# A recurrent layer and two MLPs: router products shared between VectorE and TensorE, a gate product moved to GpSimd, one operation for the decay of the states

## The chip, the cores and the metric

The kernel runs on one core of a Trainium2 chip. The core's engines work side by side, each through its own queue in order: TensorE (PE, with its weight loads as PEld), VectorE (DVE), ScalarE (ACT), GpSimd (POOL) and SyncE (SP), which only issues DMAs here. The metric is the time of one execution in microseconds (us); lower is better.

## The reference

Three layers in a row: a recurrent attention with a matrix state per head, an MLP with the activation h - tanh(h), and a mixture of eight experts in which each token goes to the expert with the largest normalised product.

```python
for t in range(S):                       # B=4, H=8, S=768, D=40
    ...
    C = f_stab * C + i_stab * np.einsum('bhd,bhe->bhde', vt, kt)
    n = f_stab[:, :, None] * n + i_stab[:, :, None] * kt
    h_tilde = np.einsum('bhde,bhe->bhd', C, qt)
    denom = np.maximum(np.abs(nq), 1.0)
    o = 1.0 / (1.0 + np.exp(-o_gate[:, :, t]))
    y[:, :, t] = o * h_tilde / denom
...
h = x @ w_in                             # x: 3072 x 320, w_in: 320 x 2048
return ((h - np.tanh(h)) @ w_out)
...
xn = x / (np.linalg.norm(x, axis=-1, keepdims=True) + 1e-06)
en = expert_emb / (np.linalg.norm(expert_emb, axis=-1, keepdims=True) + 1e-06)
logits = xn @ en.T / tau                 # 3072 x 8
expert_idx = np.argmax(logits, axis=1)
...
out[mask] = gate_w[mask, None] * (np.maximum(x[mask] @ w1[e], 0.0) @ w2[e])
```

## The kernel before, in words

The sequence of 768 is cut into six chunks of 128 (`NCH`), and a chunk of one batch is a unit, so there are 24 units i = 4c + b. Within a unit the attention is worked out for the whole chunk at once; from chunk to chunk only the states `Cst` are carried, one 40 x 41 block per head, two heads side by side in the partitions 0 to 39 and 64 to 103 (columns 0 to 40 and 41 to 81) with zeros in the other blocks.

A unit has these steps, each placed at a step of the main loop by `PLACE1` (chunk 1) and `PLACE2` (chunks 2 to 5): `parts` (split of q and k into a high part on ACT and a low part on DVE or POOL, L162), `scores` (matmuls into `ps`, L562 or L564, exponentials on ACT, a mask on POOL), `weigh` (product with the mask into `A`, L580), `outs` (matmuls into `po` and `pi`), `sums` (sums `tmp` L617 and `T` L620, the denominator `dn` with its reciprocal, the gate product `z` = sigmoid(o) x 1/dn L630, the decay of the states L640 and their update L642), `finish` (`y` = T x z, L645 and L647), `turn` (transposes of y into `px` on PE), `low` (the copy of `px` as input of the first MLP, and the store of y). `stack` copies the states in high and low parts for the next chunk (`Cl`, L162 on POOL).

The first MLP runs over the six chunks (512 tokens each) as six stages of 16 steps n, one block of 128 hidden units a step: `gemm1` (8 matmuls into one of two PSUM banks `h`), `g_chain` (u and s on ACT, L210 and L211; s and g on DVE, L212 and L213, which reads `h` and so frees the bank), `g_split` (`ghi` on ACT, `glo` on POOL), `gemm2` (12 matmuls into four banks `acc`). In step n the loop issues the split of n + 1, the chain of n + 2, `gemm2` of n and `gemm1` of n + 3. In stage c the attention of chunk c + 1 runs beside it, and the routing of chunk c - 1. After stage 5 come ten passes over the experts with 8 steps each.

The routing (`route`, then `slots`) takes the four tiles of 128 tokens of a chunk. For each it forms the squared norm on ACT and eight products with the experts' vectors: `VDOT[c]` of them on DVE (one operation each with a running sum, L263, from a copy `enb` of the vectors in every partition), the others as a product on POOL (L267) with the sum on ACT (L268). `VDOT` 0 means `dots`: the tile is transposed on PE (three matmuls into `pd`, L241), copied to `xt` (DVE L242, ACT L243), and multiplied with the transposed vectors `enT` (three matmuls, L246), and DVE copies the eight columns (L247). Chunk 5 alone does so; it is routed after stage 5. `enT` is made by `turn_en`: a load of the 8 x 320 vectors `es` into a buffer of z's tag, three transposes into one bank `pn` on PE, three copies on ACT. `slots` is a generator; each step of the main loop runs it to its next `yield`.

The instructions of the start-up are written in their order by hand; from the `|` in `START` on a scheduler orders them by its own costs, with the code's order as priority. So a change of one part can shift the order of others. The buffers of a pool's tag are used in turn, and an instruction that needs one waits for the last user of the one before.

Of the kernel before, what the change touches and what calls it, by code (L numbers as in the profile page):

```python
# [9 lines left out]
F32 = mybir.dt.float32  # L10
# [5 lines left out]
AF = mybir.ActivationFunctionType  # L16
ALU = mybir.AluOpType
# [5 lines left out]
NCH = S // L  # L23
# [4 lines left out]
E = 8  # L28
# [25 lines left out]
STACK = 12  # L54
SIGM = (2, 14)
EXPERT_X = (-3, 0)
LOAD_EW, LOAD_X, LOAD_X2, TURN_EN = 13, 4, 4, 6
KW_POOL = (0, 2, 3, 4, 5)
VDOT = (8, 8, 8, 8, 6, 0)
WARM0, WARM = 20, 2  # L60


# [48 lines left out]
def build(ctx, tc, qk, qk3, vk, og, gat, w64, w12, emb, tau, cst, tok, empty, out):  # L111
    nc = tc.nc
    V, A, G, T = nc.vector, nc.scalar, nc.gpsimd, nc.tensor
    MM = T.matmul

    const = ctx.enter_context(tc.tile_pool(name="const", bufs=1))
# [105 lines left out]
    enT = []  # L222

    def turn_en():

        e8 = attp.tile([8, 320], F32, tag="z", name="e8", bufs=1)
        nc.sync.dma_start(out=e8, in_=es)
        pn = at_bank("pn")
        enT.append(attp.tile([128, 3, 8], F32, tag="dn", name="enT"))
        for k in range(3):  # L230
            n = min(128, 320 - 128 * k)
            T.transpose(pn[0:n, 8 * k:8 * k + 8], e8[:, 128 * k:128 * k + n], ident[0:8, 0:8])
            A.activation(out=enT[0][0:n, k, :], in_=pn[0:n, 8 * k:8 * k + 8], func=AF.Copy)

    def dots(x2, lg):

        pd = at_bank("pd")
        xt = attp.tile([128, 384], F32, tag="y", name="xt")
        for k in range(3):
            n = min(128, 320 - 128 * k)  # L240
            T.transpose(pd[0:n, 128 * k:128 * k + 128], x2[:, 128 * k:128 * k + n], ident)  # L241
        V.tensor_copy(out=xt[:, 0:256], in_=pd[:, 0:256])  # L242
        A.activation(out=xt[0:64, 256:384], in_=pd[0:64, 256:384], func=AF.Copy)  # L243
        for k in range(3):
            n = min(128, 320 - 128 * k)
            MM(pd[:, 384:392], xt[0:n, 128 * k:128 * k + 128], enT[0][0:n, k, :], start=k == 0, stop=k == 2)  # L246
        V.tensor_copy(out=lg, in_=pd[:, 384:392])  # L247

    def slots(pool, nj, R, si, vdot=E, part=E):

        n = nj * 8
        ss = pool.tile([128, nj], F32, tag="ss", name="ss")
        lg = pool.tile([128, nj, 8], F32, tag="lg", name="lg")
        jk = [pool.tile([128, 320], BF16, tag=f"jk{k}", name="jk") for k in range(2)]
        for j in range(nj):
            x2 = R[:, j, 0:320]
            A.activation(out=jk[0], in_=x2, func=AF.Square, accum_out=ss[:, j:j + 1])
            if vdot == 0:
                dots(x2, lg[:, j, :])
                yield  # L260
            for e in range(E if vdot else 0):
                if e < vdot:
                    V.scalar_tensor_tensor(out=jk[1], in0=x2, scalar=1.0, in1=enb[:, e, :], op0=ALU.mult, op1=ALU.mult,  # L263
                                           accum_out=lg[:, j, e:e + 1])
                else:
                    dt = attp.tile([128, 320], F32, tag="A", name="dt")
                    G.tensor_tensor(out=dt, in0=x2, in1=enb[:, e, :], op=ALU.mult)  # L267
                    A.activation(out=jk[0], in_=dt, func=AF.Copy, accum_out=lg[:, j, e:e + 1])  # L268
                if (e + 1) % part == 0:
                    yield  # L270
        G.tensor_tensor(out=ss, in0=ss, in1=half[:, 0:nj], op=ALU.pow)
        V.tensor_scalar(out=ss, in0=ss, scalar1=1.0e-6, scalar2=None, op0=ALU.add)
        V.reciprocal(out=ss, in_=ss)
        yield
        V.tensor_scalar(out=ss, in0=ss, scalar1=itau, scalar2=None, op0=ALU.mult)
        V.tensor_tensor(out=lg, in0=lg, in1=ss.unsqueeze(2).to_broadcast([128, nj, 8]), op=ALU.mult)
        mx = pool.tile([128, nj, 1], F32, tag="mx", name="mx")
        V.tensor_reduce(out=mx, in_=lg, op=ALU.max, axis=AX.X)
        eq = pool.tile([128, nj, 8], F32, tag="eq", name="eq")
        V.tensor_tensor(out=eq, in0=lg, in1=mx.to_broadcast([128, nj, 8]), op=ALU.is_ge)  # L280
        V.tensor_tensor(out=lg, in0=lg, in1=mx.to_broadcast([128, nj, 8]), op=ALU.subtract)
        A.activation(out=lg, in_=lg, func=AF.Exp)
        wt = col(C_WT, n).rearrange("p (j e) -> p j e", j=nj)
        V.tensor_tensor(out=eq, in0=eq, in1=wt, op=ALU.mult)
        V.tensor_reduce(out=mx, in_=eq, op=ALU.max, axis=AX.X)
        V.tensor_tensor(out=eq, in0=wt, in1=mx.to_broadcast([128, nj, 8]), op=ALU.is_equal)
        oh = pool.tile([128, nj, 8], BF16, tag="oh", name="oh")
        pre = pool.tile([128, nj, 8], BF16, tag="pre", name="pre")
        V.tensor_copy(out=oh, in_=eq)
        V.tensor_copy(out=pre[:, 0, :], in_=carry)  # L290
        for j in range(1, nj):
            V.tensor_tensor(out=pre[:, j, :], in0=pre[:, j - 1, :], in1=oh[:, j - 1, :], op=ALU.add)
        V.tensor_tensor(out=carry, in0=pre[:, nj - 1, :], in1=oh[:, nj - 1, :], op=ALU.add)
        yield
        pr = at_bank("pr")
        MM(pr[:, 0:n], trib, oh.rearrange("p j e -> p (j e)"), start=True, stop=False)
        MM(pr[:, 0:n], oneb, pre.rearrange("p j e -> p (j e)"), start=False, stop=True)
        gs = pool.tile([128, nj, 1], F32, tag="gsum", name="gsum")
        V.tensor_reduce(out=gs, in_=lg, op=ALU.add, axis=AX.X)
        V.tensor_scalar(out=gs, in0=gs, scalar1=1.0e-9, scalar2=None, op0=ALU.add)  # L300
        V.reciprocal(out=R[:, :, 320:321], in_=gs)
        sl = pool.tile([128, nj, 8], F32, tag="sl", name="sl")
        V.tensor_tensor(out=sl, in0=pr[:, 0:n].rearrange("p (j e) -> p j e", j=nj),
                        in1=col(C_EOFF, n).rearrange("p (j e) -> p j e", j=nj), op=ALU.add)
        V.tensor_tensor(out=sl, in0=sl, in1=eq, op=ALU.mult)
        V.tensor_reduce(out=mx, in_=sl, op=ALU.add, axis=AX.X)
        V.tensor_copy(out=si, in_=mx.rearrange("p j o -> p (j o)"))
        yield
# [63 lines left out]
    attp = p1.enter_context(tc.tile_pool(name="attp", bufs=2))  # L372
# [3 lines left out]
    Cst = attp.tile([104, 16, 82], F32, tag="C", name="C", bufs=1)  # L376
    gts = {}
    units = {}
    sig = {}
# [3 lines left out]
    eGL = attp.tile([104, NCH * 16], F32, tag="eGL", name="eGL", bufs=1)  # L383
# [143 lines left out]
    def attention(c):  # L527
# [3 lines left out]
        def unit(b):  # L531
            i = c * B + b
# [76 lines left out]
            def sums():  # L609
# [5 lines left out]
                if c:  # L615
                    Tt = v['T'] = attp.tile([128, 8, 41], F32, tag="T", name="T", bufs=1)
                    V.tensor_tensor(out=tmp, in0=po[:, 0:w * 8].rearrange("p (h d) -> p h d", h=8)[:, :, 0:41],  # L617
                                    in1=eG[:, 8 * i:8 * i + 8].unsqueeze(2).to_broadcast([128, 8, 41]),
                                    op=ALU.mult)
                    V.tensor_tensor(out=Tt.rearrange("p h d -> p (h d)"), in0=pi[:, 0:328],  # L620
                                    in1=tmp.rearrange("p h d -> p (h d)"), op=ALU.add)
                else:
                    Tt = v['T'] = pi[:, 0:328].rearrange("p (h d) -> p h d", h=8)
                dn = attp.tile([128, 8, 1], F32, tag="dn", name="dn")
# [2 lines left out]
                V.tensor_tensor(out=dn, in0=nq, in1=dn, op=ALU.max)  # L627
                V.reciprocal(out=dn, in_=dn)
                z = v['z'] = attp.tile([128, 8, 40], F32, tag="z", name="z", bufs=1)
                (V if c > 1 else G).tensor_tensor(out=z, in0=sig[i].rearrange("p (h d) -> p h d", h=8),  # L630
                                                  in1=dn.to_broadcast([128, 8, 40]), op=ALU.mult)
                if c == 0:
                    for par in range(2):
                        p0, c0 = 64 * par, 41 * par
                        A.activation(out=Cst[p0:p0 + 40, 4 * b:4 * b + 4, c0:c0 + 41], in_=st[p0:p0 + 40, :, :],
                                     func=AF.Copy)
                for par in range(2 if 0 < c < NCH - 1 else 0):
                    p0, c0 = 64 * par, 41 * par
                    Cv = Cst[p0:p0 + 40, 4 * b:4 * b + 4, c0:c0 + 41]
                    V.tensor_tensor(out=Cv, in0=Cv, in1=eGL[p0:p0 + 40, 4 * i:4 * i + 4].unsqueeze(2)  # L640
                                    .to_broadcast([40, 4, 41]), op=ALU.mult)
                    V.tensor_tensor(out=Cv, in0=Cv, in1=st[p0:p0 + 40, :, :], op=ALU.add)  # L642
            def finish():
                y = v['y'] = attp.tile([128, 384], F32, tag="y", name="y")
# [30 lines left out]
        for b in range(B if c else 0):  # L675
            n = 16 * (c - 1) - 4 + 4 * b
# [140 lines left out]
    NS = NCH * NF  # L817
# [8 lines left out]
    for word in START.split():  # L826
        op, k = word[0], word[1:]
# [126 lines left out]
            sp[n] = relu_chain(hs.pop(n), rows_of(step(n)[0])[3])  # L954

    def special(n, c, f, rx):
        if n == NS - TURN_EN:
            turn_en()
        if n == NS - NF - 4:
            ranking()  # L960
# [34 lines left out]
    for n in range(NS + NE):  # L995
        c, f, ps = step(n)
# [51 lines left out]
        elif f == NFE - 1:  # L1048
            ti, gt = exT[c][3:5]
            for j, bank in enumerate(acc.pop(('e', c))):  # L1050
# [4 lines left out]
                        in_=ob[0:m], in_offset=None, bounds_check=NT - 1, oob_is_err=False)  # L1055
# [26 lines left out]
    with tc.If(reg > CAP):  # L1082
        X = gp.tile([128, XW], F32, tag="X", name="X")
        xt = gp.tile([128, 3, 128], F32, tag="xt", name="xt")
# [150 lines left out]
```

## Time and profile before

| what | value |
| --- | --- |
| time of the runs | 851.04 us median of 3 (850.98 to 857.43) |
| the profiled execution | 854.08 us, span 852.1 us from first to last instruction |
| mean granted TensorE clock | 0.927 of full speed |
| busy, share of the span | PE 90%, PEld 80%, DVE 75%, ACT 58%, POOL 43% |
| stages 0 to 5 begin at (first matmul of `gemm1`) | 58.8, 162.4, 262.6, 360.0, 451.6, 536.2 us |
| the expert passes' first `gemm1` | 611.0 us |

The stretches in the tables run from one of these starts to the next. A row of busy time counts the time in which at least one instruction of the engine ran; matmuls overlap each other, and at the lower of the two clock levels they take longer, so a busy PE is not the same as a PE at full speed. A row of waits names the instruction that waited, the one that released it, the sum in us, the number of times and the longest.

### The profile page before, as it was taken

To read this page: it belongs to the slowest core of one execution; us is meant where nothing else is said; L and a number is where in the kernel's file an instruction comes from. 1 tells how busy PE (TensorE), PEld (TensorE's weight loads), DVE (VectorE), ACT (ScalarE), POOL (GpSimd) and SP (SyncE) were. 2 spreads that over 40 slices of the span, in tenths; PEclk is the share of its full clock that TensorE was granted. 3 is DMA by queue.
4 is the path that set the end of the run, shared out by engine and by line. 5 is a ranking of instruction groups with operands and counts; after the bars stand their busy time and mean duration, and the time that the engine had idled before them with its cause. 6 is when DMAs were issued, how large, how long until landed. Compare 5 with 4: busy or idle time off the path is not lost. (4 is left out here: it accounts for less than half of the span.)

```text
span 852.1 us, 14301 instructions
## 1 busy us (share of the span) xinstructions
PE 763.0 (90%) x4640; PEld 677.6 (80%) x4640; DVE 638.1 (75%) x1417; ACT 496.1 (58%) x1175; POOL 364.3 (43%) x375
## 2 busy tenths in 40 slices
PE   8979899797899898998889989888899999999994
PEld 5767778686788687787778778767799989999994
DVE  6476999898887989879986999797473775556420
ACT  3775787767557645685558634655554655455421
POOL 2383677657463554655463525443522111012111
PEclk8558998988989989999999999999999999999998
DMA  8574766543344243432335311201535764455000
GB/s 273 211 254 160 257 220 198 133 122 93 87 126 131 82 101 87 143 105 79 89 109 152 92 34 44 73 1 51 177 115 164 232 181 140 120 173 165 36 20 21
DMA packets 60756, 107.55 MB, mean 126 GB/s; under 512 B 24958, under 2 KB 33321, under 8 KB 60016
## 3 DMA queue, kind: packets, MB, share of 16 engines
q1 hardware_dynamic: 57968, 98.46, 38.8%
q0 software_dynamic: 2512, 7.89, 2.5%
q8 instruction: 38, 0.62, 0.3%
q14 instruction: 46, 0.38, 0.1%
q10 hardware_dynamic: 192, 0.20, 0.1%
HBM read 92.91 MB, written 17.87 MB: 130 GB/s over the span
## 5 line engine op out<-in xcount | busy, mean ns | idle before, releaser
L185 PE MATMUL h<-xh,wi 128*128 128x512 f32 (+6 forms) x880 | 303.3, 382 | 18.8 <-DVE g L213 13.3
L185 PEld LDWEIGHTS h<-xh,wi 128*128 128x128 f32 x880 | 171.7, 198 | 45.7 <-DVE g L213 17.3
L193 PE MATMUL acc<-wo,ghi 128*128 128x320 f32 (+1 forms) x616 | 200.6, 326 | 0.0
L162 POOL TENSOR_TENSOR glo<-g,ghi 128x512 fp32r<-128x512 f32 x96 | 133.2, 1389 | 156.6 <-ACT ghi L218 119.8
L185 PE MATMUL h<-xl,wi 128*128 128x512 f32 (+6 forms) x528 | 197.7, 379 | 0.4
L195 PE MATMUL acc<-wo,glo 128*128 128x320 f32 (+1 forms) x616 | 194.9, 317 | 2.0 <-POOL glo L162 2.0
L194 PE MATMUL acc<-wo,ghi 128*128 128x320 f32 (+1 forms) x616 | 194.7, 316 | 0.0
L218 ACT ACTIVATE ghi<-g 128x512 fp32r<-128x512 f32 x96 | 60.2, 628 | 111.7 <-DVE g L213 94.6
L193 PEld LDWEIGHTS acc<-wo,ghi 128*128 128x128 f32 (+1 forms) x616 | 118.4, 192 | 6.1 <-ACT D L568 1.3
L195 PEld LDWEIGHTS acc<-wo,glo 128*128 128x128 f32 (+1 forms) x616 | 117.7, 191 | 4.0 <-POOL glo L162 3.2
L194 PEld LDWEIGHTS acc<-wo,ghi 128*128 128x128 f32 (+1 forms) x616 | 118.1, 192 | 3.2
L185 PEld LDWEIGHTS h<-xl,wi 128*128 128x128 f32 x528 | 105.0, 199 | 12.3 <-DVE xl L660 1.6
L212 DVE SCALAR_TENSOR_TENSOR s<-s,u 128x512 f32<-128x512 f32 x96 | 78.9, 822 | 41.8 <-ACT s L211 40.2
L263 DVE SCALAR_TENSOR_TENSOR jk<-R,enb 128x320 bf16<-128x320 f32 x152 | 96.5, 635 | 2.7 <-ACT R L727 1.7
L156 POOL DMA_INDIRECT out<-ob,ti x29 | 28.5, 982 | 156.9 <-ACT ob L1053 133.3
L929 DVE SCALAR_TENSOR_TENSOR glo<-h,ghi 128x256 fp32r<-128x256 f32 (+5 forms) x80 | 41.4, 517 | 60.0 <-ACT ghi L928 54.5
L568 ACT ACTIVATE D<-D,bcol 128x128 f32<-128x128 f32 x192 | 64.6, 390 | 33.6 <-DMA D<-gd 33.3
L928 ACT ACTIVATE ghi<-h 128x256 fp32r<-128x256 f32 (+5 forms) x80 | 36.7, 458 | 65.4 <-PE acc L194 55.9
L162 DVE TENSOR_TENSOR wi<-ew,wi 128x256 fp32r<-128x256 f32 (+1 forms) x128 | 50.1, 392 | 31.4 <-ACT wi L174 29.8
L211 ACT ACTIVATE s<-u,cs 128x512 f32<-128x512 f32 x96 | 68.7, 716 | 0.9
L213 DVE SCALAR_TENSOR_TENSOR g<-s,h 128x512 f32<-128x512 f32 x96 | 65.4, 682 | 2.9
L210 ACT ACTIVATE u<-h 128x512 f32<-128x512 f32 x96 | 55.9, 583 | 12.6 <-PE h L185 11.3
(192 smaller groups left out, 1199.5 us busy)
## 6 DMA issues: line engine op xcount, KB each, us to landing
ew<-in_w SPq DMA_DIRECT2D x64, 352.0 KB
W<-in_qk SPq DMA_DIRECT2D x32, 480.0 KB
D<-gd SPq DMA_DIRECT2D x48, 256.0 KB
raw<-in_w SPq DMA_DIRECT2D x16, 704.0 KB
vk<-in_vk SPq DMA_DIRECT2D x20, 324.0 KB
xs<-blank SPq DMA_DIRECT2D x32, 161.0 KB
sg<-in_og SPq DMA_DIRECT2D x6, 640.0 KB
ys<-y SPq DMA_DIRECT2D x24, 160.0 KB
```

The lines of the kernel that those rows point to most:

```text
L162: eng.tensor_tensor(out=out, in0=x, in1=hi.bitcast(F32), op=ALU.subtract)
L185: MM(h[:, 0:cols], wi[:, k, :], x[:, kk, :], start=n == 0, stop=n == len(seq) - 1)
L193: MM(o, ghi[:, sl], wo[:, 0, 0:320], start=first, stop=False)
L194: MM(o, ghi[:, sl], wo[:, 1, 0:320], start=False, stop=False)
L195: MM(o, glo[:, sl], wo[:, 0, 0:320], start=False, stop=last)
L210: A.activation(out=u, in_=h, func=AF.Square, accum_out=usum[:, n:n + 1])
L211: A.activation(out=s, in_=u, func=AF.Square, bias=col(C_BETA))
L212: V.scalar_tensor_tensor(out=s, in0=s, scalar=GAMMA, in1=u, op0=ALU.add, op1=ALU.mult)
L213: V.scalar_tensor_tensor(out=g, in0=s, scalar=C2, in1=h, op0=ALU.mult, op1=ALU.mult)
L218: A.activation(out=ghi, in_=g, func=AF.Copy)
L263: V.scalar_tensor_tensor(out=jk[1], in0=x2, scalar=1.0, in1=enb[:, e, :], op0=ALU.mult, op1=ALU.mult, accum_out=lg[:, j, e:e + 1])
L568: A.activation(out=Dt[:, j, :], in_=Dt[:, j, :], func=AF.Exp, bias=bcol[:, k:k + 1])
```

## The change

Five edits. In the chunks 0 to 4 the tiles 0 and 2 of the four now go through `dots`, the tiles 1 and 3 have all eight products on DVE (`VDOT[4]` is 8 instead of 6, so nothing is left for POOL and ACT there); a tile in `dots` has one `yield` instead of two. Since `enT` is needed from chunk 0's routing on, `turn_en` stands at step 12 instead of step 90, and `enT` has a buffer of its own. The larger copy to `xt` is ACT's instead of DVE's. The product `z` is on POOL for all chunks (before: chunks 0 and 1). The decay of a unit's states is one operation over 104 partitions and both halves of the columns instead of one for each block of 40 partitions.

```diff
-LOAD_EW, LOAD_X, LOAD_X2, TURN_EN = 13, 4, 4, 6
+LOAD_EW, LOAD_X, LOAD_X2, TURN_EN = 13, 4, 4, 12
 KW_POOL = (0, 2, 3, 4, 5)
-VDOT = (8, 8, 8, 8, 6, 0)
+VDOT = (8, 8, 8, 8, 8, 0)
...
-        enT.append(attp.tile([128, 3, 8], F32, tag="dn", name="enT"))
+        enT.append(const.tile([128, 3, 8], F32, tag="enT", name="enT"))
...
-        V.tensor_copy(out=xt[:, 0:256], in_=pd[:, 0:256])
+        A.activation(out=xt[:, 0:256], in_=pd[:, 0:256], func=AF.Copy)
         A.activation(out=xt[0:64, 256:384], in_=pd[0:64, 256:384], func=AF.Copy)
...
-            if vdot == 0:
+            on_pe = vdot == 0 or part < E and j % 2 == 0
+            if on_pe:
                 dots(x2, lg[:, j, :])
                 yield
-            for e in range(E if vdot else 0):
+            for e in range(0 if on_pe else E):
...
-                (V if c > 1 else G).tensor_tensor(out=z, in0=sig[i].rearrange("p (h d) -> p h d", h=8),
+                G.tensor_tensor(out=z, in0=sig[i].rearrange("p (h d) -> p h d", h=8),
...
+                if 0 < c < NCH - 1:
+                    Cu = Cst[:, 4 * b:4 * b + 4, :]
+                    V.tensor_tensor(out=Cu, in0=Cu, in1=eGL[:, 4 * i:4 * i + 4].unsqueeze(2).to_broadcast([104, 4, 82]), op=ALU.mult)
                 for par in range(2 if 0 < c < NCH - 1 else 0):
...
-                    V.tensor_tensor(out=Cv, in0=Cv, in1=eGL[p0:p0 + 40, 4 * i:4 * i + 4].unsqueeze(2)
-                                    .to_broadcast([40, 4, 41]), op=ALU.mult)
                     V.tensor_tensor(out=Cv, in0=Cv, in1=st[p0:p0 + 40, :, :], op=ALU.add)
...
-        if n == NS - TURN_EN:
+        if n == TURN_EN:
             turn_en()
```

Below, the order of the instructions at three places, first before and then after. A row is line, operation, output<-inputs and shape; lines after the edits are shifted by one or two (L263 becomes L264, L630 L631, L645 L647).

PE in the fourth step of stage 2, in `gemm2` (L193 to L195, banks `acc`), before:

```order
L194 MATMUL acc_2948<-wo,ghi 128x320
L195 MATMUL acc_2948<-wo,glo 128x320
L193 MATMUL acc_2949<-wo,ghi 128x320
L194 MATMUL acc_2949<-wo,ghi 128x320
L195 MATMUL acc_2949<-wo,glo 128x320
L193 MATMUL acc_2950<-wo,ghi 128x320
L194 MATMUL acc_2950<-wo,ghi 128x320
L195 MATMUL acc_2950<-wo,glo 128x320
L185 MATMUL h<-xh,wi 128x512
```

And after, where the third tile of chunk 1 goes through `dots`:

```order
L194 MATMUL acc_2955<-wo,ghi 128x320
L195 MATMUL acc_2955<-wo,glo 128x320
L241 MATMUL pd<-cs,R 128x128 x2
L241 MATMUL pd<-cs,R 64x128
L193 MATMUL acc_2956<-wo,ghi 128x320
L194 MATMUL acc_2956<-wo,ghi 128x320
L195 MATMUL acc_2956<-wo,glo 128x320
L193 MATMUL acc_2957<-wo,ghi 128x320
L194 MATMUL acc_2957<-wo,ghi 128x320
L246 MATMUL pd<-enT,xt 128x8 x3
L195 MATMUL acc_2957<-wo,glo 128x320
L185 MATMUL h<-xh,wi 128x512
```

Transposes and products stand inside `gemm2`, five of its matmuls apart, and `gemm1` (L185) follows.

DVE at the end of a unit's `sums` in stage 1 (dn the denominator, q the low parts of a later unit's q), before:

```order
L627 TENSOR_TENSOR dn<-T,dn 128x8
L642 TENSOR_TENSOR C<-C,po 40x4x41
L628 RECIPROCAL dn<-dn 128x8
L162 TENSOR_TENSOR q_2410<-W,q_2410 40x512
L630 TENSOR_TENSOR z<-sg,dn 128x320
L162 TENSOR_TENSOR q_2488<-W,q_2488 40x512
L645 TENSOR_TENSOR y<-T,z 128x320
L212 SCALAR_TENSOR_TENSOR s<-s,u 128x512
```

And after:

```order
L628 TENSOR_TENSOR dn<-T,dn 128x8
L162 TENSOR_TENSOR q_2441<-W,q_2441 40x512
L629 RECIPROCAL dn<-dn 128x8
L162 TENSOR_TENSOR q_2528<-W,q_2528 40x512
L647 TENSOR_TENSOR y<-T,z 128x320
L304 TENSOR_TENSOR sl<-pr,cs 128x32
L649 COPY y<-y 128x64
```

z has left this queue; y follows the reciprocal with one operation between. On POOL z stands after:

```order
L162 TENSOR_TENSOR glo<-g,ghi 128x512
L162 TENSOR_TENSOR Cl<-C,C_1612 40x164
L631 TENSOR_TENSOR z<-sg,dn 128x320
L156 DMA xs<-R,si 24576x322 x4
L162 TENSOR_TENSOR glo<-g,ghi 128x512
```

It has come in between the low parts `Cl` of the states and `glo` (L156 are the scatters of the routing).

PE at step 12, in the last `gemm2` rows of that step (px the transposes of y of the last unit of chunk 1), after; before, these rows hold neither pn nor its waits, and `turn_en` stood in stage 5:

```order
L195 MATMUL acc_761<-wo,glo 128x320
L232 MATMUL pn<-cs,e_1646 128x8
L655 MATMUL px<-cs,y 128x128 x3
L193 MATMUL acc_762<-wo,ghi 128x320
L232 MATMUL pn<-cs,e_1646 128x8
L194 MATMUL acc_762<-wo,ghi 128x320
L195 MATMUL acc_762<-wo,glo 128x320
L232 MATMUL pn<-cs,e_1646 64x8
L185 MATMUL h<-xh,wi 128x512
```

The three transposes of `turn_en` now stand between matmuls of `gemm2`, the first of them ahead of px.

## Rows read from the trace of the kernel before

**Rows 1.** Busy time by stretch, whole core, stages 1 to 5 in order:

```profile
core 0: us, PE busy (x) PEld busy (x) DVE busy (x) ACT busy (x) POOL busy (x), PEclk, DMA share, GB/s
...
162.38:262.64 100.26, 86.83 (x529) 77.14 (x528) 85.45 (x197) 62.38 (x150) 59.95 (x59) 0.90 0.41 113
262.64:360.01 97.37, 84.97 (x529) 74.64 (x528) 84.41 (x193) 60.19 (x141) 51.19 (x50) 0.93 0.38 103
360.01:451.62 91.61, 82.28 (x528) 72.27 (x528) 82.95 (x185) 60.16 (x141) 47.97 (x48) 0.96 0.38 103
451.62:536.17 84.55, 76.13 (x457) 66.38 (x456) 74.67 (x184) 49.54 (x113) 36.40 (x29) 1.00 0.25 72
536.17:610.95 74.78, 65.00 (x332) 54.43 (x333) 57.19 (x131) 44.15 (x113) 35.04 (x33) 0.98 0.18 57
```

**Rows 2.** Waits of PE, stage 1 (waiter, releaser, us, times, longest):

```profile
PE ps L564 <- DVE q L162: 9.3, 2, 5.3
PE ps L564 <- DVE k L162: 2.3, 2, 1.8
```

**Rows 3.** The same view, engine PE, stage 4:

```profile
PE ps L564 <- DVE k L162: 2.5, 3, 1.1
```

**Rows 4.** The same view, engine PE, stage 5:

```profile
PE h L185 <- DVE g L213: 7.8, 7, 3.3
...
PE pn L232 <- ACT enT L233: 1.1, 1, 1.1
```

**Rows 5.** Busy time of L263 alone (products on DVE) in stages 1 to 5:

```profile
162.38:262.64 100.26, 19.19 (x64) 0.90 0.41 113
262.64:360.01 97.37, 18.89 (x64) 0.93 0.38 103
360.01:451.62 91.61, 22.43 (x64) 0.96 0.38 103
451.62:536.17 84.55, 20.68 (x64) 1.00 0.25 72
536.17:610.95 74.78, 16.56 (x48) 0.98 0.18 57
```

**Rows 6.** Groups of instructions by shape, whole run (xcount, busy us, mean ns):

```profile
L640 DVE TENSOR_TENSOR C<-C,eGL 40x164 f32<-40x164 f32 x32 | 17.3, 540 | 5.8 <-PE po L592 4.7 <-POOL Cl L162 0.6
...
L617 DVE TENSOR_TENSOR tmp<-po,eG 128x328 f32<-128x328 f32 x20 | 9.9, 493 | 2.9 <-remote 2.2 <-PE po L596 0.6
...
L630 DVE TENSOR_TENSOR z<-sg,dn 128x320 f32<-128x320 f32 x16 | 12.7, 795 | 0.2
...
L630 POOL TENSOR_TENSOR z<-sg,dn 128x320 f32<-128x320 f32 x8 | 7.2, 894 | 12.4 <-DVE dn L628 12.4
```

**Rows 7.** L645 in stage 0, then whole run: duration ns min/median/max, who waited:

```profile
L645 DVE TENSOR_TENSOR y<-T,z x4: 809/1278/1559, 82.0 to 154.7; 128x320 f32<-128x320 f32 x4
...
  PE px L653: 4.7, 2
...
L645 DVE TENSOR_TENSOR y<-T,z x20: 475/491/1574, 82.0 to 531.0; 128x320 f32<-128x320 f32 x20
```

**Rows 8.** L212 and L213 in the whole run: duration ns min/median/max:

```profile
L212 DVE SCALAR_TENSOR_TENSOR s<-s,u x96: 672/686/1783, 65.7 to 610.1; 128x512 f32<-128x512 f32 x96
...
L213 DVE SCALAR_TENSOR_TENSOR g<-s,h x96: 669/681/690, 66.9 to 611.1; 128x512 f32<-128x512 f32 x96
```

**Rows 9.** Timeline around chunk 5's products on PE (start us, us, engine, what):

```profile
621.15 0.81 PE L241 MATMUL pd<-cs,R 128*128 128x128 f32 x6
...
622.84 0.93 PE L246 MATMUL pd<-enT,xt 128*128 128x8 f32 x6
...
624.22 0.17 DVE L247 COPY lg<-pd 128x8 f32<-128x8 f32 x1 [1.12 <-ACT wo L175]
```

**Rows 10.** Timeline of SP's queue at the write and re-read of es:

```profile
60.20 0.29 SPq L719 DMA_DIRECT2D es<-em  x1
...
64.25 0.32 SPq L720 DMA_DIRECT2D enb<-es  x1
```

## The prediction, made before the changed kernel was timed

> **What bounds the kernel now.** I read the table of stretches first, because the change acts on five of them. A stage is sixteen steps of the first MLP, cut at the first matmul of `gemm1` (L185) of every sixteenth step. Look at PE's column and the clock beside it [rows 1]. Stage 1 lasts 100.3 us with PE busy for 86.8 at a granted clock of 0.90, that is partly at 1.2 instead of 2.4 GHz. A clock that is 0.10 short costs at most 0.10 x 100.3 = 10.0 us, so the same PE work at full clock needs about 76.8 us. I call this the floor and the rest, 23.5 us, the excess. The same sum gives floors of 78.2, 78.6, 76.1 and 63.5 us for stages 2 to 5 and excesses of 19.2, 13.0, 8.4 and 11.3.
>
> DVE's column says where the excess comes from. DVE is busy for 85.5, 84.4, 83.0, 74.7 and 57.2 us [rows 1]; divided by the floor that is 1.11, 1.08, 1.06, 0.98 and 0.90. The excess falls with this ratio until about 1 and then stays near 8 to 11. The waits of PE agree: in stage 1 the scores (L564) wait 9.3 and 2.3 us for DVE's low parts of q and k [rows 2], of 13.4 us that PE is idle at all (100.26 - 86.83). In stage 4 the largest is still a DVE wait, 2.5 us [rows 3]. In stage 5, where no attention is left, `gemm1` waits 7.8 us for g (L213), because its PSUM bank comes free only behind DVE's queue [rows 4]. So stages 1 to 3 are bound by a DVE that works through more than PE does; stages 4 and 5 by PE with stalls in the pipeline. The expert passes behind stage 5 are not touched.
>
> **The change part by part.**
>
> *Products.* L263 takes 19.2, 18.9, 22.4 and 20.7 us of DVE in stages 1 to 4 for 32 products each, and 16.6 us for 24 in stage 5 (the count in the rows includes the read of each sum) [rows 5]. Two of four tiles leave DVE, so half goes in stages 1 to 4: 9.6, 9.4, 11.2 and 10.3 us. In stage 5 `VDOT` rises from 6 to 8 for the tiles that stay, so 24 become 16 and 5.5 us go, and with them eight products on POOL and eight sums on ACT, which nobody waited for long. Two copies of 0.17 us per stage come in (L247) [rows 9].
>
> *The same products on TensorE.* Chunk 5 already does this, so the price is in the trace: six transposes, two tiles', in 0.81 us, and one tile's three products, each recorded twice, in 0.93 us [rows 9]. One tile costs 0.81 / 2 + 0.93 = 1.34 us of PE, two tiles 2.7 us a stage. This is added to the floors of all five stages. The two copies of the transposed tile now both run on ACT; the order puts five products of `gemm2` between transposes and products to cover them. I take the cover as enough; without it each tile stalls PE, which is the third rival.
>
> *Decay of the states.* 32 operations of 540 ns become 16 over 104 partitions and 328 columns [rows 6]. That shape is not in the trace as such. 493 ns is what L617 takes for 328 columns with one input in PSUM [rows 6]; an operation with both inputs in SBUF is stretched at times (L212 against L213 [rows 8]), so I take 0.7 us, between 0.49 and twice 0.54. 17.3 - 16 x 0.7 = 6 us of DVE, about 2 us in each of stages 0 to 2, where the decays of four chunks lie (bounds: 17.3 - 16 x 1.08 = 0, and 17.3 - 16 x 0.49 = 9.4).
>
> *Gate product z on POOL.* It takes 795 ns on DVE and 894 ns on POOL [rows 6]. But DVE does not simply win 16 x 0.8 us. Where z is on POOL already (stage 0), the y behind it takes 1278 ns in the median against 491 ns over the run [rows 7]. 795 - (1278 - 491) is zero, so I take nothing for DVE and 1 us in total for later y's. The reason shows elsewhere too: L212, with both inputs in SBUF, is stretched from 686 to as much as 1783 ns, while L213, which has one input in PSUM, never leaves 669 to 690 [rows 8]. The Trainium skill, SBUF — State Buffer, section "SBUF: two separate sides", says that a DVE operation with two SBUF inputs and a GpSimd operation exclude each other for a whole instruction. By that rule moving z to POOL frees no DVE time, and the trace agrees; whoever credits DVE with the full 12.7 us, and PE with all of it, comes to about 820 instead of 834.
>
> *Turning the experts' vectors (`turn_en`) early.* Its load of 10 KB now waits on SP for y of the last unit of chunk 1, because it takes z's only buffer; behind it on SP wait that unit's store of y, which waits for the same y anyway, and a load of W. PE meets the first transpose between two banks of `gemm2`, ahead of that unit's px, and must wait for the load. The nearest row: es is written from 60.20 and its re-read, which needs it landed, is issued at 64.25, so such a transfer lands within 4.1 us [rows 10]. Two turnarounds with ACT follow, 1.1 us where PE waited for one [rows 4]. Bounds 0 and 6.3; I take +3 in stage 0. In stage 5 the 1.1 us go.
>
> **Sum.** DVE falls to 74.2, 73.3, 72.1, 64.7 and 52.0 us, at most 0.93 of the new floors (79.5, 80.9, 81.3, 78.8, 66.2). Below a ratio of 1 the trace shows an excess of 8.4 (stage 4), so I give this to stages 1 to 3, which also means that almost no time at the low clock is left there. Stage 4 has a seventh less DVE work before its waits: 7.0. Stage 5 loses 1.1 and a part of its waits for g: 9.0. New stages: 87.9, 89.3, 89.7, 85.8, 75.2, against before -12.4, -8.1, -1.9, +1.3, +0.4; together -20.7. With +3 for `turn_en` and +1 for z: -17. The profiled execution took 854.1 us (span 852.1), the median of the runs is 851.0; 17 us off the median is **834 us**.
>
> The gain sits in stages 1 and 2. What is late next is PE itself: 80 of 88 us in each stage.
>
> **Bounds.** If less DVE work also halves the excess of stage 4, to 4.2, and that of stage 5 to 5.6, and `turn_en` and z cost nothing, the stages give 83.7, 85.1, 85.5, 83.0 and 71.8: -39.5, about 811. If the excess falls only half the way to 8.4 (16.0, 13.8, 10.7), stays in stage 4 and is 10.2 in stage 5, they give 95.5, 94.7, 92.0, 87.2, 76.4: -2.8, and with `turn_en` at 6 it is 854.
>
> **Rivals.**
>
> *z's new path takes the relief back (no change).* Before, reciprocal, z and y followed each other on DVE. Now DVE reaches y while z stands in POOL's queue behind `glo` and `Cl`, and px on PE needs y. In stage 0 this cost PE 4.7 us in four units [rows 7], 1.2 us each; sixteen units more would cost 19 us, so 834 + 19 - 1 = 852. For it: POOL is busy for 60 of 100 us in stage 1, and the stage will be shorter. Its y is longer there as well: 16 x (1278 - 491) ns is 12.6 us ahead of px, 834 - 1 + 12.6 = 846 by that alone [rows 7]. Against it: stage 0 also has the weights' conversion on DVE, and one other operation still stands between reciprocal and y. The lock of the Trainium skill (the page and section named above) would stretch y in just this way, since T and z both lie in SBUF and POOL starts its next operation right after z; the y's of stage 0 agree.
>
> *More relief than I take (the lower bound).* The pipeline stalls themselves come from DVE's queue, so they shrink as well: 811.
>
> *PE waits for ACT in every tile (slower).* ACT works in order and is busy for 62 of 100 us in stage 1 [rows 1]; its copies of the transposed tile can stand behind an operation that waits for DVE's g. PE's queue then stands at the products with enT, and all of `gemm1` and `gemm2` with it. Ten tiles are moved. From 2.6 us a tile on the kernel is slower by 1% (834 + 26 = 860); at 3 us, after which PE would again come back at the low clock, 864 or more. Against it: where PE waited for ACT's copies of enT it was 1.1 us [rows 4], and five products stand between.
>
> The change can't fail to take place: the instructions are there in the order. What could miss is only their effect.
>
> **How the numbers follow.** A measurement of this kernel tells 1% (8.5 us) from no change: below 842.5 is faster, above 859.5 slower. My forecast, with its neighbourhood down to 815, has 0.53; the lower bound's case 0.07; z's path 0.25 (no change); PE behind ACT 0.15 (slower). Faster 0.60, no change 0.25, slower 0.15. The range goes from 808, below the lower bound, to 860, where the slow case begins; I leave out some 0.03 below and 0.13 above.
>
> **What would show it.** Right: L264 (L263 before) has half its instructions in stages 1 to 4 and DVE drops by 10 to 13 us in each; stages 1 and 2 shrink by 8 to 12 us each, stages 4 and 5 hardly; the clock in stages 1 and 2 rises to 0.95 or more; `ps` waits little for q and k. The second rival's sign is px waiting for y, with y behind z of POOL, over 10 us in all. The slow one's is pd (L246) waiting for xt of ACT for over 2 us a tile. `turn_en` shows as one wait of PE for the load of e8 near the end of stage 0. I am wrong in the mechanism if DVE falls as said and the stages 1 and 2 keep their length: then PE's waits on DVE were not a matter of DVE's load but of the order in its queue.

## The result: 0.9% slower, with far less work on VectorE

The changed kernel takes 861.08 us in the median of ten runs (857.11 to 864.24), the kernel before 851.83 us beside it (849.38 to 857.43). The ratio is 1.0091 with a 95% interval of 1.0072 to 1.0109. The forecast was 834 in a range from 808 to 860, so the median lies just above the range; by the bound of 1% the ratio is still "no change", at its slower edge. The profiled execution took 858.88 us, span 857.2 us.

The profile after, busy time by stretch for the stages 0 to 5 in order (columns as in [rows 1]):

```profile
59.32:167.78 108.46, 94.70 (x563) 80.76 (x562) 87.85 (x137) 76.67 (x179) 71.45 (x73) 0.91 0.64 207
167.78:266.82 99.04, 89.35 (x525) 79.50 (x525) 68.15 (x155) 59.23 (x148) 54.54 (x56) 0.85 0.38 108
266.82:363.16 96.34, 87.12 (x546) 77.81 (x546) 66.33 (x155) 60.72 (x144) 51.52 (x53) 0.89 0.37 101
363.16:458.71 95.55, 86.24 (x546) 76.73 (x546) 65.85 (x151) 60.86 (x145) 50.69 (x51) 0.93 0.39 103
458.71:543.49 84.78, 81.22 (x475) 72.67 (x474) 61.76 (x149) 50.94 (x116) 36.92 (x32) 0.94 0.23 66
543.49:617.09 73.60, 63.46 (x346) 54.73 (x346) 54.63 (x129) 44.45 (x108) 26.90 (x26) 1.00 0.28 90
```

Read DVE's column (the third with a count) against [rows 1]: it falls by 17.3, 18.1, 17.1, 12.9 and 2.6 us in stages 1 to 5, by more than the forecast in the first four. Then read the lengths: stages 1, 2 and 5 are only 1.2, 1.0 and 1.2 us shorter, stage 3 is 3.9 and stage 0 4.9 us longer. Stages 0 and 1 have to be read together, because the cut between them has moved: two steps of `gemm2`, 24 matmuls, now lie ahead of it. The count of L193, one of the three lines of `gemm2`, shows it (PE and PEld, stages 0 and 1, before and then after):

```profile
58.80:162.38 103.58, 18.83 (x56) 11.41 (x56) 0.89 0.63 208
162.38:262.64 100.26, 21.78 (x64) 13.24 (x64) 0.90 0.41 113
...
59.32:167.78 108.46, 21.88 (x64) 13.03 (x64) 0.91 0.64 207
167.78:266.82 99.04, 19.69 (x56) 11.83 (x56) 0.85 0.38 108
```

Together the two stages take 207.5 us instead of 203.8. The clock fell instead of rising, from 0.90 and 0.93 to 0.85 and 0.89 in stages 1 and 2. The prediction had named this case: DVE falls and the stages keep their length, so the order in DVE's queue decides, not its load.

The waits of DVE in stage 1 after (waiter, releaser, us, times, longest) show what it stands at:

```profile
DVE R L730 <- DMA xs<-R,si: 8.1, 1, 8.1
DVE s L212 <- ACT s L211: 6.7, 5, 2.7
...
DVE y L647 <- POOL z L631: 5.2, 3, 3.3
```

The first row is new. L730 (L728 before) is a copy of four columns, the token numbers, into the tile `R` of the next chunk's routing. This is the copy in the whole run after:

```profile
L730 DVE COPY R<-cs x6: 156/172/172, 153.9 to 612.9; 128x4 f32<-128x4 f32 x6
its engine sat idle before it (us, times) until:
  DMA xs<-R,si: 26.4, 4
```

The same view of before has no idle time under L728:

```profile
L728 DVE COPY R<-cs x6: 160/165/173, 157.7 to 617.9; 128x4 f32<-128x4 f32 x6
```

The tag "raw" that `R` uses has two buffers, and the stacked states `C3` hold one as long as they are needed, so the two are not used in turn. The next `R` goes where the previous `R` lay, and its first writer waits until POOL's four scatters `xs<-R,si` (L156) have landed. In before the copies for chunks 1 to 3 have the same wait, but they stand 15 rows behind the conversion of the row numbers (L307) that starts the scatters of the chunk before. In stage 1 DVE comes to the copy 7.0 us after the last scatter's issue has ended, and stands for nothing (timeline of before, DVE and the last scatter on POOL):

```profile
245.38 0.31 DVE L307 CAST si<-mx 128x4 uint32<-128x4 f32 x1
...
250.20 0.97 POOL L156 DMA_INDIRECT xs<-R,si  x1 [0.30 <-issue]
...
258.20 0.17 DVE L728 COPY R<-cs 128x4 f32<-128x4 f32 x1
```

The copy for chunk 4 stands 4 rows behind and waits for no transfer, since it got the other buffer. In after the copies for chunks 1 to 4 all have the wait and stand 5 rows behind that conversion (L308). A tile in `dots` has one `yield` instead of two, and the routing ends earlier, 64 us into stage 1 instead of 83. Why the scheduler then leaves 5 rows and not 15 is not shown. DVE's order with some of its waits, after, from the end of chunk 0's routing in stage 1:

```
L308 CAST si<-mx 128x4 [waits DVE_49]
L213 SCALAR_TENSOR_TENSOR g<-s,h 128x512 [waits DVE_49]
L581 TENSOR_TENSOR A<-ps,D 128x512 [waits PE_49]
L162 TENSOR_TENSOR k_2529<-W,k_2529 40x512
L662 TENSOR_TENSOR xl<-px,xh 128x3x128
L730 COPY R<-cs 128x4 [waits DMASW2_49,DMASW3_49,DMASW1_49,DMASW0_49]
L212 SCALAR_TENSOR_TENSOR s<-s,u 128x512
L213 SCALAR_TENSOR_TENSOR g<-s,h 128x512
```

Now the same place in time, after, timeline of PE, POOL (last scatter) and DVE (start, us, engine, what, idle before it and releaser):

```profile
235.04 0.40 PE L185 MATMUL h<-xh,wi 128*128 128x512 f32 x1
235.27 0.40 PE L185 MATMUL h<-xl,wi 128*128 128x512 f32 x1
...
236.49 0.97 POOL L156 DMA_INDIRECT xs<-R,si  x1 [0.30 <-issue]
...
238.81 0.41 PE L195 MATMUL acc<-wo,glo 128*128 128x320 f32 x1 [1.92 <-POOL glo L162]
...
243.10 0.17 DVE L730 COPY R<-cs 128x4 f32<-128x4 f32 x1 [8.05 <-DMA xs<-R,si]
243.20 0.69 DVE L212 SCALAR_TENSOR_TENSOR s<-s,u 128x512 f32<-128x512 f32 x1
243.93 0.69 DVE L213 SCALAR_TENSOR_TENSOR g<-s,h 128x512 f32<-128x512 f32 x1
...
244.67 0.79 PE L185 MATMUL h<-xh,wi 128*128 128x512 f32 x1 [3.10 <-DVE g L213]
...
246.12 0.63 PE L185 MATMUL h<-xl,wi 128*128 128x512 f32 x1
246.54 0.63 PE L185 MATMUL h<-xh,wi 128*128 128x512 f32 x1
...
259.53 0.44 PE L185 MATMUL h<-xl,wi 128*128 128x512 f32 x1
259.81 0.39 PE L185 MATMUL h<-xh,wi 128*128 128x512 f32 x1
```

The four scatters end on POOL at 237.46 and DVE goes on at 243.10. Behind the copy wait s and g, g frees the bank that `gemm1` needs, and PE loses 3.1 us there. The stop of 1.9 us ahead of it is not the copy's: `glo` stood on POOL behind the scatters. PE loses more behind the two: two rows of `gemm1` are 0.23 us apart ahead of the stops and 0.42 us behind them, that is the lower level of the clock, and so it stays until 259.5. The first run below shows the same place without the copy's stop.

Two smaller costs show. The load for `turn_en` is issued at 159.38 and PE makes the first transpose at 165.29, with px behind it. PE does not stand for the load: it comes straight from a row of `gemm2`. ACT stands for the transpose, and DVE for ACT's copy of px, which `gemm1` of the next stage reads:

```profile
159.38 0.42 SPq L227 DMA_DIRECT2D e<-es  x1
...
164.90 0.47 PE L195 MATMUL acc<-wo,glo 128*128 128x320 f32 x1
165.29 0.27 PE L232 MATMUL pn<-cs,e 8*128 8x8 f32 x1
...
165.60 0.18 ACT L233 ACTIVATE enT<-pn 128x8 f32<-128x8 f32 x1 [1.65 <-PE pn L232]
...
167.49 0.56 DVE L662 TENSOR_TENSOR xl<-px,xh 128x384 fp32r<-128x384 f32 x1 [4.85 <-ACT xh L660]
```

And DVE waits for POOL's z, 18.5 us in 16 waits in the whole run (1.8 in 3 before). The group of z and of y (L647; L645 in [rows 7]) in after:

```profile
L631 POOL TENSOR_TENSOR z<-sg,dn 128x320 f32<-128x320 f32 x24 | 20.4, 852 | 19.5 <-DVE dn L629 15.5 <-PE pd L241 2.3 <-PE acc L195 1.0
...
L647 DVE TENSOR_TENSOR y<-T,z 128x320 f32<-128x320 f32 x20 | 19.2, 958 | 18.0 <-POOL z L631 17.9
```

### The profile page after: what moved, and what is told of

The parts are those of the page before. It is cut to its first block, busy times and chain, and to the rows that moved or that the text cites. A ratio compares the mean times of both kernels' runs of the same rounds, so it can differ in the third digit from the quotient of the medians.

```text
span 857.2 us, 14347 instructions
## 1 busy us (share of the span) xinstructions
PE 777.2 (91%) x4727; PEld 697.0 (81%) x4730; DVE 562.4 (66%) x1247; ACT 499.7 (58%) x1183; POOL 359.3 (42%) x383
## 5 line engine op out<-in xcount | busy, mean ns | idle before, releaser
L185 PE MATMUL h<-xh,wi 128*128 128x512 f32 (+6 forms) x880 | 302.7, 382 | 20.3 <-DVE g L213 16.7
L185 PEld LDWEIGHTS h<-xh,wi 128*128 128x128 f32 x880 | 172.4, 199 | 45.8 <-DVE g L213 19.5
L195 PE MATMUL acc<-wo,glo 128*128 128x320 f32 (+1 forms) x616 | 197.9, 322 | 10.0 <-POOL glo L162 9.9
L193 PE MATMUL acc<-wo,ghi 128*128 128x320 f32 (+1 forms) x616 | 203.5, 330 | 1.6 <-ACT ghi L218 1.6
L185 PE MATMUL h<-xl,wi 128*128 128x512 f32 (+6 forms) x528 | 198.1, 380 | 0.1
L194 PE MATMUL acc<-wo,ghi 128*128 128x320 f32 (+1 forms) x616 | 197.1, 320 | 0.0
L195 PEld LDWEIGHTS acc<-wo,glo 128*128 128x128 f32 (+1 forms) x616 | 119.5, 194 | 13.0 <-POOL glo L162 12.3
L193 PEld LDWEIGHTS acc<-wo,ghi 128*128 128x128 f32 (+1 forms) x616 | 119.5, 194 | 5.0 <-ACT ghi L218 2.2
L194 PEld LDWEIGHTS acc<-wo,ghi 128*128 128x128 f32 (+1 forms) x616 | 119.7, 194 | 2.8
L185 PEld LDWEIGHTS h<-xl,wi 128*128 128x128 f32 x528 | 105.8, 200 | 11.2 <-DVE xl L662 0.4
L212 DVE SCALAR_TENSOR_TENSOR s<-s,u 128x512 f32<-128x512 f32 x96 | 76.1, 793 | 55.8 <-ACT s L211 55.4
L156 POOL DMA_INDIRECT out<-ob,ti x29 | 28.8, 995 | 151.3 <-ACT ob L1055 130.1
L213 DVE SCALAR_TENSOR_TENSOR g<-s,h 128x512 f32<-128x512 f32 x96 | 65.6, 683 | 3.0
L570 POOL TENSOR_SCALAR_AFFINE_SELECT D<-D 128x512 f32<-128x512 f32 x48 | 35.6, 742 | 65.1 <-ACT D L569 61.4
```

The source lines that it names most:

```text
L185: MM(h[:, 0:cols], wi[:, k, :], x[:, kk, :], start=n == 0, stop=n == len(seq) - 1)
L193: MM(o, ghi[:, sl], wo[:, 0, 0:320], start=first, stop=False)
L194: MM(o, ghi[:, sl], wo[:, 1, 0:320], start=False, stop=False)
L195: MM(o, glo[:, sl], wo[:, 0, 0:320], start=False, stop=last)
L212: V.scalar_tensor_tensor(out=s, in0=s, scalar=GAMMA, in1=u, op0=ALU.add, op1=ALU.mult)
L213: V.scalar_tensor_tensor(out=g, in0=s, scalar=C2, in1=h, op0=ALU.mult, op1=ALU.mult)
```

## The experiments

Each time is the median of its runs, each ratio is to the kernel before on the same chip, with its 95% interval. The stages are those of the profiled execution.

**The token copy later, in the changed kernel.** The column is written behind the reciprocal that fills the column beside it, when `slots` has run. The value is the same.

```diff
-        V.tensor_copy(out=R[:, :, 321], in_=cs[:, C_TOK + c * B:C_TOK + c * B + NJ])
         yield
         si = attp.tile([128, NJ], U32, tag="si", name="si")
         yield from slots(wk, NJ, R, si, VDOT[c], 4)
+        V.scalar_tensor_tensor(out=R[:, :, 321], in0=R[:, :, 320], scalar=0.0,
+                               in1=cs[:, C_TOK + c * B:C_TOK + c * B + NJ], op0=ALU.mult, op1=ALU.add)
```

> The token column of R is written behind the reciprocal instead of at the start of the routing, so that DVE no longer stands at it until the scatters of the chunk before have landed (8.1, 6.6, 7.2 and 4.6 us in stages 1 to 4 of the changed kernel). Theory 1 (a DVE queue that waits for the scatters takes the relief back): those four waits are gone, DVE's busy time stays near 66 us in stages 1 to 3, and the kernel takes 836 to 846 us. Theory 2 (the stages are held by the order in the queues of ACT, POOL and PE, and another wait follows at once): 855 to 863 us, as the changed kernel.

Measured: 842.96 us, 0.9877 [0.9836, 0.9919]; against the changed kernel's 1.0091 that is 2.1%, some 18 us. Its stages 1 and 2:

```profile
168.30:257.00 88.70, 81.78 (x524) 72.69 (x524) 68.84 (x153) 57.71 (x147) 55.35 (x56) 0.94 0.42 117
257.00:349.50 92.50, 83.88 (x547) 74.26 (x546) 69.07 (x155) 61.04 (x145) 52.86 (x54) 0.96 0.39 107
```

DVE works as much as in after (68.8 and 69.1 us), but the stages are 10.3 and 3.8 us shorter and the clock is 0.94 and 0.96. No wait of DVE for the scatters is left (POOL still stands 5.6 us for them, in 3 rows), and `gemm1`'s waits for g in the whole run fall from 16.7 us to 3.8. At the place shown above, PE has the stop at `glo` as before, and the clock falls behind it too; but the stop for g is gone, and from 242.12 on two rows of `gemm1` are 0.25 us apart again:

```profile
238.57 0.50 PE L195 MATMUL acc<-wo,glo 128*128 128x320 f32 x1 [2.36 <-POOL glo L162]
...
241.27 0.63 PE L185 MATMUL h<-xh,wi 128*128 128x512 f32 x1
241.70 0.61 PE L185 MATMUL h<-xl,wi 128*128 128x512 f32 x1
242.12 0.41 PE L185 MATMUL h<-xh,wi 128*128 128x512 f32 x1
242.37 0.39 PE L185 MATMUL h<-xl,wi 128*128 128x512 f32 x1
```

So there the copy cost the stop of 3.1 us and most of the time at the lower level, some 20 us in after and under 4 us here. One copy of 0.17 us at the wrong place in the queue turned a gain into a loss.

**The vectors for `turn_en` loaded early.** They go into a buffer of their own at the end of the start-up; the turn itself stays at step 12.

```diff
-        e8 = attp.tile([8, 320], F32, tag="z", name="e8", bufs=1)
-        nc.sync.dma_start(out=e8, in_=es)
+        e8 = e8s[0]
```

> The experts' vectors are loaded at the end of the start-up into a buffer of their own, the turn at step 12 stays. Theory 1 (the 4.9 us by which stage 0 grew are the load that waits for z's buffer and PE behind it): stage 0 comes back to 103 to 105 us, the kernel takes 854 to 858 us. Theory 2 (stage 0 grew for another reason, z or the order): stage 0 stays at 107 to 109 us and the time within 2 us of the changed kernel.

Measured: 853.31 us, 0.9986 [0.995, 1.0022]. That is 1.05% (9 us) less than the change. Stage 0 goes from 108.5 to 102.6 us, but the two steps of `gemm2` lie in stage 1 again; stages 0 and 1 together go from 207.5 to 202.1 us. Stages 2 and 3 do not get shorter (98.7, 95.6), and DVE's wait for the scatters is 26.5 us in 4: it stays when the late load goes.

**z back on DVE from chunk 2 on**, in the changed kernel (`(V if c > 1 else G).tensor_tensor(out=z, ...`).

> z is back on DVE for the chunks 2 to 5, the rest is as in the changed kernel. Theory 1 (z's path costs little; DVE had room): within 4 us of the changed kernel. The rival of the prediction (DVE stands at y until POOL has made z, 18.5 us in all, and px waits behind it): 10 us or more faster than the changed kernel, 843 to 851 us.

Measured: 847.08 us, 0.9891 [0.9836, 0.9946], so 2.0% (17 us) less than the change. The wait for the scatters stays (24.8 us in 4). Moving z to POOL cost time by itself, here more than below.

**One after the other.** The late token copy with the early load:

> The late token column and the early load together. Theory 1: the two add up, 831 to 842 us, which is faster than the kernel before. Theory 2: 850 to 860 us.

Measured: 839.4 us, 0.981 [0.9757, 0.9863]; stages 102.6, 93.1, 93.9, 90.3, 85.5, 72.2. With the early load the cut between stages 0 and 1 lies where it lay in before. The load is worth 0.7% (5.7 us) on top by the medians, but the intervals overlap and the two profiled executions have the same span, 838.0 us, so that is not clear of noise. With z on DVE as well:

> Late token column, early load of the experts' vectors, and z back on DVE for the chunks 2 to 5; what is left of the change are the products on TensorE, the decay in one operation and the copy on ACT. Theory 1 (z on POOL costs on its own, because DVE and px wait for it): 6 to 12 us faster than with z on POOL, 826 to 836 us. Theory 2 (z back on DVE only moved the order, so that it gains nothing once the wait for the scatters is gone): 836 to 846 us.

Measured: 830.93 us, 0.9746 [0.9726, 0.9766]; stages 102.2, 94.8, 90.8, 89.6, 83.5, 72.3. z is worth another 0.6% (5.4 us; these intervals too overlap, by 0.0009). One by one in the changed kernel the three repairs gave 2.1, 1.05 and 2.0%, together they give 3.45%, so the costs overlap. What is left of the change here, the products, the decay and ACT's copy, is a gain of 2.5%, some 21.6 us.

**The products back on DVE**, with z on POOL and the new decay kept and the token copy at its old place:

```diff
-            on_pe = vdot == 0 or part < E and j % 2 == 0
+            on_pe = vdot == 0
```

(`VDOT[4]` is 6 and `turn_en` runs late again.)

> All tiles of chunks 0 to 3 have their products on DVE again (chunk 4: six on DVE and two on POOL, as before), the turn stands in stage 5 again; z on POOL and the decay in one operation stay. No move of the token column: with the longer routing it comes later by itself. Theory 1: no wait of DVE for the scatters; z on POOL costs 5 to 12 us and the decay gives back a few, so 853 to 864 us, no faster than the kernel before. Theory 2 (the products on TensorE are what costs, the rest helps): 838 to 848 us.

Measured: 852.71 us, 1.0001 [0.998, 1.0022]. DVE waits for no scatter, and the copies for chunks 1 to 3 stand 15 rows behind the conversion again, so that wait came with the products' edit and its shorter routing. y waits 9.5 us in 15 for z; that this loss and the gain of the decay (below) cancel is argued, not shown.

**The late token copy in the kernel before.**

> The kernel before with the late token column alone. There DVE never waited for the scatters, so theory 1 expects no change: 846 to 856 us, within 1% of the kernel before. Theory 2 (the late column helps for another reason, such as a better order): 8 us or more faster.

Measured: 855.0 us, 1.0027 [0.9999, 1.0056]. The edit by itself brings nothing where the copy did not wait; the 18 us above are the repair of a damage.

**All four tiles of the chunks 0 to 4 through `dots`**, in the version with the three repairs:

```diff
-            on_pe = vdot == 0 or part < E and j % 2 == 0
+            on_pe = vdot == 0 or part < E
```

> As late_e8_z, but all four tiles of the chunks 0 to 4 go through TensorE. DVE loses another 10 us a stage, PE gains another 2.7 us a stage. Theory 1 (DVE is no longer what bounds once half of the products are gone; PE is): 3 to 12 us slower than late_e8_z. Theory 2 (DVE's load still sets the stages): 5 us or more faster than late_e8_z.

Measured: 822.79 us, 0.9664 [0.9633, 0.9696], 0.8% less than with two tiles and the fastest of all. Its stages 3 and 4:

```profile
345.70:433.50 87.80, 84.09 (x565) 75.04 (x564) 62.81 (x125) 62.14 (x149) 46.51 (x48) 0.98 0.41 112
433.50:512.80 79.30, 78.49 (x493) 71.11 (x492) 57.46 (x124) 52.30 (x121) 34.39 (x29) 1.00 0.26 76
```

In stage 4 PE is busy for 78.49 of 79.30 us at full clock: here PE is the bound, in the sense of its busy time. The theory that PE had become the bound with two tiles, and would lose by four, fell.

**The same with z on POOL.**

> As all_dots, with z on POOL again as in the change. If z on POOL costs because DVE stands at y while POOL makes z: the cost stays, 4 to 8 us slower than all_dots, with waits of DVE y for POOL z of 8 us or more. If it cost only because DVE was loaded: within 3 us of all_dots.

Measured: 833.23 us, 0.9756 [0.9711, 0.9802], so z on POOL costs 0.9% (about 8 us). The waits for z in the whole run (releaser, us, times), with z on POOL:

```profile
  POOL z L631: 14.4, 16
```

On DVE, in the run before this one:

```profile
  POOL z L631: 3.0, 3
```

**The decay in two operations again**, in the version with the three repairs and two tiles:

```diff
+                    V.tensor_tensor(out=Cv, in0=Cv, in1=eGL[p0:p0 + 40, 4 * i:4 * i + 4].unsqueeze(2)
+                                    .to_broadcast([40, 4, 41]), op=ALU.mult)
```

(in place of the one operation on `Cu`)

> As late_e8_z, with the decay in two operations again. If the decay gives what the prediction took (6 us of DVE in stages 0 to 2, most of it passed on in stages 1 and 2): 2 to 6 us slower than late_e8_z. If the decay lies in time that DVE has to spare anyway: within 2 us of it.

Measured: 839.15 us, 0.9812 [0.9763, 0.986] against 0.9746, so the merged decay is worth about 0.7% (5.6 us) by the medians; the two intervals just touch. In the profiled executions stage 0 is 3.5 us longer, but stage 1 is 1.5 us shorter where the expectation had most of the loss.

**The larger `xt` copy on DVE again**, same version:

> As late_e8_z, with the larger copy of the transposed tile on DVE as before the change. If PE waits for ACT's order there (the slow rival of the prediction): 3 us or more faster. If the copy is covered on either engine: within 3 us.

Measured: 838.91 us, 0.9796 [0.9748, 0.9844]. Not faster, so ACT's second copy is not what costs. By the medians it is 0.5% (4.3 us) slower, more than the 3 us that the expectation allowed; the intervals overlap a little, so whether the copy on ACT helps stays open.

## Why the prediction was wrong

**The step that failed** is the first of the part by part, the products. It counted what leaves DVE, half of the products, and that held. It did not follow the routing's other instructions, which a shorter `slots` moves ahead. DVE's copy L728 had a wait that cost nothing in 15 rows; at 5 rows it cost 26.4 us of DVE and, by the run with the late copy, 18 us of time. That is more than the forecast gain of 17. With this wait the second step fails too, that a stage with DVE below 1 of PE's floor has an excess of 8.4. By the same sum the floor of stage 1 after is 89.35 - 0.15 x 99.04 = 74.5 us, DVE's share of it 0.91 and the excess 24.5, against 23.5 before. Nor do the repairs bring 8.4 back. With all three, stage 1, which there holds as much of `gemm2` as before, has the row

```profile
162.00:256.80 94.80, 86.80 (x546) 78.40 (x546) 71.93 (x161) 63.85 (x156) 53.07 (x57) 0.89 0.45 122
```

that is a floor of 76.4 us, 0.94 of it on DVE, and an excess of 18.4. The ratio says how long a queue is, not where in it something stands.

**What was right, in part by luck.** `ps` waits 1.4 us for k and none for q in stage 1, where it waited 2.3 and 9.3 [rows 2]. The sum of the stages comes out in the repaired version: without the three costs the stages 1 to 5 sum to 431.1 us against 448.6 before: -17.5 where the sum had -20.7, and the median is 21 us lower (830.93 against 852.02). The place was off: -5.5, -6.6, -2.0, -1.0, -2.5 in stages 1 to 5, where the sum had -12.4, -8.1, -1.9, +1.3 and +0.4. So the sum agrees in part by luck: the forecast had too much gain in stage 1 and none in stages 4 and 5. Stage 1 there still runs at a clock of 0.89.

**`turn_en`** was taken at 3 us between 0 and 6.3; by the medians it measured 9 in the kernel as changed, where stages 0 and 1 together were 5.4 us shorter without it, and 5.7, not clear of noise, beside the late token copy. The one wait of PE for the load that was to show it is not there. With the load early the three transposes come at 151.26 to 152.93, more than 3 us ahead of px; after, they stand around px behind two more steps of `gemm2`. So the load moved the order more than it stopped PE; what each cost was not separated.

**z on POOL** was taken at 1 us; it measured 17 in the kernel as changed, 5.4 in the repaired one and 8 with four tiles. The first rival had its mechanism, y behind z in POOL's queue, and with 18 us its price for the kernel as changed. Its way was another, though. The y's take 19.2 us in after against 17.2 with z back on DVE, 2 us and not the 12.6 of the lock. Nor is it px: PE's waits for y fell (8.7 us in 4, before 11.3 in 7). The y stands in DVE's queue, 18.5 us in 16 waits, and holds up what is behind it. With z back on DVE, and nothing else changed:

```profile
L647 DVE TENSOR_TENSOR y<-T,z 128x320 f32<-128x320 f32 x20 | 17.2, 859 | 2.5 <-POOL z L631 2.3
L631 DVE TENSOR_TENSOR z<-sg,dn 128x320 f32<-128x320 f32 x16 | 12.8, 797 | 0.4
```

The busy time of the whole run, with z back on DVE and then after:

```profile
PE 771.2 (91%) x4730; PEld 692.5 (82%) x4730; DVE 568.2 (67%) x1263; ACT 499.6 (59%) x1183; POOL 346.2 (41%) x367
...
PE 777.2 (91%) x4727; PEld 697.0 (81%) x4730; DVE 562.4 (66%) x1247; ACT 499.7 (58%) x1183; POOL 359.3 (42%) x383
```

So z's 12.8 us leave DVE, but its busy time falls by 5.8 us only (5.9 and 4.8 in the two other pairs of runs). The rest comes back as longer operations, 2 us of it in y. The forecast took nothing for DVE, since y would grow by as much as z took; about half of z's time came back, most of it not in y. So DVE was relieved a little, and the kernel still lost by it.

**The decay** was right in size: 0.7 us an operation and 6 us of DVE were taken, 0.717 and 17.3 - 11.5 = 5.8 measured, in the row

```profile
L640 DVE TENSOR_TENSOR C<-C,eGL 104x328 f32<-104x328 f32 x16 | 11.5, 717 | 3.9 <-POOL Cl L162 2.3 <-PE po L593 1.7
```

of after. They lie in stages 1 and 2 (3.1 and 2.7 us) and not in stage 0, where 2 were taken. The time for it, 5.6 us by the medians, is near that, but just at the edge of the noise.

**Two tiles on PE** were taken at 2.7 us a stage, which is too much. Stage 4 has a clock of 1.00 before and in the version with four tiles: PE is busy for 76.13 us [rows 1] and 78.49, 2.4 us for four tiles, 0.6 a tile where 1.34 was taken (some matmul records can be missing, so this is rough). The row of products in [rows 9] was one tile by itself; inside `gemm2` it overlaps its neighbours.

**PE behind ACT**, the slow rival, was not borne out. PE waited 11.7 us in 11 for `xt` in after, 1.1 a time where the rival needed 2.6, and giving the copy back to DVE won nothing.

The time ended at the edge of the slow rival's, but at a place that no rival named.

Open: a third buffer for `R`, 5 KB a partition, should take the wait away at its root and was not run. Stage 3, 3.9 us longer after with a wait of 7.2 us in it, takes 90.4 us with the late copy, 1.2 us less than before, so its length needs no other cause.

## What to carry to other kernels

Where an edit shortens a chain of work that takes turns with others, look in the changed order at the first instruction of the next turn: which buffer it takes, who must let go of it, and how many rows now lie between. A wait that is covered today is a price tomorrow, and on an engine that works in order it is paid by all that stands behind it. Giving work to an idle engine can lose although the busy one is relieved, if the busy one must wait in its queue for the answer.

## What the runs showed of the hardware that was not expected

The scatters take long to let go: four of 128 rows were issued on POOL between 232.44 and 237.46, and the buffer was free at 243.10, 5.6 us after the last issue ended. In stages 2 to 4 it took 4.3, 4.4 and 1.8 us.

A small operation on DVE can stand for the whole of a row of POOL operations. In the kernel before, the 128 x 8 operation L626, 168 ns in the median, once took 4214 ns, from 251.44 to 255.65:

```profile
251.44 4.21 DVE L626 TENSOR_SCALAR dn<-T 128x8 f32<-128x8 f32 x1
```

On POOL at that time six operations ran without a gap; the first and the last of them:

```profile
251.17 0.65 POOL L569 TENSOR_SCALAR_AFFINE_SELECT D<-D 128x512 f32<-128x512 f32 x1
...
254.34 1.28 POOL L162 TENSOR_TENSOR glo<-g,ghi 128x512 fp32r<-128x512 f32 x1
```

The last ends at 255.62, 0.03 us before L626 does. With all four tiles in `dots` the same operation (L627 there) stood twice so, 4.52 and 4.40 us, over the same six operations of POOL. The trace counts DVE as busy all that time, so busy time on DVE isn't all work. The Trainium skill, SBUF — State Buffer, section "SBUF: two separate sides", has a lock between the two engines that is held for a whole instruction. No run here shows that the lock is the cause; if it is, the loser can stand through six instructions in a row.
